# Linear attention and a long convolution in one kernel: normalising on the query exponentials, and the signal's spectrum stored by column group

## The chip, the cores and the metric

The kernel runs on one core of a Trainium2 chip, alone. The metric is the device time of one execution in microseconds. Engines are named as in the profile: PE (TensorE matmul) and PEld (its weight load), DVE (VectorE), ACT (ScalarE), POOL (GpSimd) and SP (SyncE, here only a queue that issues DMAs). One profiled execution gives the trace from which the single durations come.

## The reference

Two independent results are written side by side, 448 columns each, for 2048 rows.

```python
# A: linear attention, 16 heads of 28, softmax feature maps
qkv = (x @ wqkv) split into q, k, v per head
pq, pk = q @ w_phi, k @ w_phi                       # per head, 28 x 28
phi_q = concat(softmax(pq), softmax(-pq))           # over 28, bf16
phi_k = concat(softmax(pk), softmax(-pk))
kv = sum over rows of phi_k^T v ;  z = sum over rows of phi_k
o = (phi_q @ kv) / (phi_q . z + 1e-6)
a = o (heads concatenated) @ wo
# B: a diagonal state space model as a convolution
K[d, l] = Re sum_n C[d,n] * exp(dt[d]*A[d,n]*l) * dt[d]*B[d,n]      # 256 states, l < 2048
y = irfft(rfft(u padded to 4096) * rfft(K padded to 4096))[:2048] + u * Dskip
out = concat(a, y, axis=-1)
```

`exp(-pq)` and `exp(pq)` are each summed over the 28 features of a head, and the two halves of `phi_q` share one denominator; so a head's output of a row is two products of raw exponentials with `kv`, each times a scale of that row, head and half.

## The kernel before

**The planner.** The program is a list of units: each is a group of instructions with an engine (or two engines, of which the planner picks one), a cost, and what it reads and writes. `Plan.run` (line 214) goes through a simulated time with a list of units that are ready on each engine. It starts the unit that can start first; among those that can start within 0.02 us it takes the lowest rank from the table `RANKS` (line 105). `PHASES` (line 141) orders the stretches of ACT that need the same activation table. The result is a fixed order of instructions on each engine; on the chip every engine runs its own list in order and waits on semaphores. `copy` (line 439) evicts PSUM or copies SBUF on ACT or DVE, as the planner chooses; `tt` (line 416) is a product or sum of two tensors on DVE; `dma` (line 457) is given the queues from which the planner may choose. All SBUF tiles lie at fixed byte addresses in one large tile, so that tiles share memory by address, and the planner takes a later writer after all earlier readers.

**Stages.** B's kernel K is made from tables: eight chunks k of 56 channels, each with complex rotations (`rot`, sines on ACT), dampings (`exps`, exponentials on ACT, multiplied in by `damp` on DVE, two products and a negation `neg`), tables of high powers (`hi`, DVE) and `build`, a matmul of the two. Results of chunks 0 to 3, 4 to 5 and 6 to 7 are the column groups 0, 1 and 2 (224, 112 and 112 of the 448 columns); `scatter_k` (line 896, steps `sc0` to `sc2`) copies each group into `Kt` by some 44 small DMAs between SBUF places. `kernel_spectrum` (steps `ks`) transforms it with DFT tables `F`, streamed from DRAM through a ring of buffers.

`signal_spectrum` (line 672, steps `us`) transforms u early, in two blocks of 1024 rows; each of 16 steps evicts 128 x 896 numbers into one of two staging buffers `sg` and stores them to the DRAM tile `SUd` by one DMA. Late in the kernel `load_su` (line 973, steps `su0` to `su2`) loads them back by column group. For group 0 that reads pieces of 448 bytes of `SUd`, for groups 1 and 2 pieces of 224. Group 0's target `SUs[0]` is at `oU`, where the tables `U` of the even chunks were; it waits until chunk 6 is built. `conv_group` (line 1015) multiplies the two spectra on DVE (11 products and sums and 7 more per group), `skip` multiplies u (`UD`, loaded by four DMAs, here at `oEQ`) by Dskip, and `inverse` transforms back on PE with tables `GI`, adding u by an identity matmul.

**The attention.** Steps `key0` to `key15` accumulate `kv` and `z` on PE; `keyend` masks them into block-diagonal tiles `KVN` and `KVZ`. `query` (line 836) handles 512 rows at a time, sc = 0 to 3:

- `qe`: the projected queries are exponentiated on ACT, both signs, into `EQ` (112 x 2 halves x 4 groups of four heads x 512 rows). Channels are on partitions. Even and odd sc have a buffer each, at `oEQ` and `oG1`.
- `qz`: a matmul gives, with rows on partitions, the sum of exponentials and the product with z of each head and half. Five small DVE instructions turn these into the scales `SC` (128 rows x 4 x 2 x 16 heads, fp32).
- `q`, four times per sc, 128 rows each: eight matmuls give the unscaled products with rows on partitions, in two PSUM tiles (one per half). DVE multiplies each by the scales, spread over the 28 channels of a head, into bf16 tiles. Eight matmuls against the identity transpose the two and add them; the sum is evicted, four matmuls multiply by `wo`, and the result is evicted and stored.

Of the kernel before, what the change touches and what calls it, by code (L numbers as in the profile page):

```python
# [18 lines left out]
D_HEAD = 28  # L19
# [80 lines left out]
def pair_rows(x2, row, t, col):  # L100
# [4 lines left out]
RANKS = {"in": 76, "inAre": 129, "inAim": 160, "inCre": 137, "inBre": 274, "inCim": 272, "inBim": 280, "inx0": 84,  # L105
         "inx1": 209, "inx2": 217, "inx3": 227, "inqk": 141, "inG": 164, "inv_": 281, "one": 67, "pid": 139, "bd":
         124, "dt": 198, "stAre": 19, "stAim": 18, "amp": 265, "hl": 238, "cs128": 177, "cs32": 202, "cs64": 161,
         "stCre": 14, "stBre": 260, "stCim": 8, "stBim": 140, "cb": 230, "H32": 98, "H64": 35, "pw": 57, "xT0": 277,
         "xT1": 190, "xT2": 121, "xT3": 0, "fold1": 135, "fold0": 235, "vones": 49, "late0": 24, "late1": 259,
         "late2": 15, "zero": 206, "ua0.0": 147, "ab0.0": 136, "ua0.1": 143, "ab0.1": 59, "ua0.2": 123, "ab0.2": 148,  # L110
         "ua0.3": 252, "ab0.3": 88, "us0.0": 215, "us0.1": 3, "us0.2": 5, "us0.3": 30, "us0.4": 50, "us0.5": 219,
         "us0.6": 203, "us0.7": 48, "exps0": 271, "rot0": 70, "hi0.0": 42, "hi0.1": 192, "hi0.2": 46, "hi0.3": 105,
         "hi0.4": 263, "hi0.5": 196, "exps1": 257, "rot1": 183, "hi1.0": 34, "hi1.1": 81, "hi1.2": 37, "hi1.3": 110,
         "hi1.4": 158, "hi1.5": 261, "damp0": 233, "neg0": 207, "build0.0": 65, "build0.1": 255, "ua1.0": 131,
         "ab1.0": 269, "ua1.1": 16, "ab1.1": 226, "ua1.2": 248, "ab1.2": 106, "ua1.3": 78, "ab1.3": 182, "us1.0": 33,
         "us1.1": 166, "us1.2": 68, "us1.3": 262, "us1.4": 234, "us1.5": 97, "us1.6": 126, "us1.7": 1, "key0": 225,
         "key1": 80, "key2": 171, "key3": 239, "key4": 253, "key5": 167, "key6": 151, "key7": 91, "exps2": 276,
         "rot2": 77, "hi2.0": 178, "hi2.1": 61, "hi2.2": 29, "hi2.3": 279, "hi2.4": 231, "hi2.5": 111, "damp1": 211,
         "neg1": 107, "build1.0": 113, "build1.1": 28, "exps3": 201, "rot3": 208, "hi3.0": 267, "hi3.1": 174, "hi3.2":
         115, "hi3.3": 157, "hi3.4": 243, "hi3.5": 218, "damp2": 240, "neg2": 132, "build2.0": 138, "build2.1": 237,  # L120
         "key8": 216, "key9": 133, "key10": 118, "key11": 173, "key12": 89, "key13": 36, "key14": 116, "key15": 93,
         "keyend": 146, "exps4": 176, "rot4": 205, "hi4.0": 223, "hi4.1": 108, "hi4.2": 153, "hi4.3": 63, "hi4.4": 26,
         "hi4.5": 47, "damp3": 40, "neg3": 23, "build3.0": 128, "build3.1": 125, "kt5": 244, "sc0": 247, "exps5": 32,
         "rot5": 258, "hi5.0": 275, "hi5.1": 254, "hi5.2": 199, "hi5.3": 212, "hi5.4": 270, "hi5.5": 7, "damp4": 52,
         "neg4": 79, "build4.0": 200, "build4.1": 163, "qe0": 117, "qz0": 104, "q0.0": 112, "q0.1": 142, "q0.2": 222,
         "q0.3": 144, "qe1": 96, "qz1": 92, "q1.0": 11, "q1.1": 134, "q1.2": 31, "q1.3": 69, "exps6": 22, "rot6": 94,
         "hi6.0": 189, "hi6.1": 56, "hi6.2": 12, "hi6.3": 246, "hi6.4": 43, "hi6.5": 188, "damp5": 169, "neg5": 38,
         "build5.0": 159, "build5.1": 175, "sc1": 229, "exps7": 213, "rot7": 250, "hi7.0": 273, "hi7.1": 266, "hi7.2":
         85, "hi7.3": 102, "hi7.4": 120, "hi7.5": 165, "damp6": 75, "neg6": 64, "build6.0": 194, "build6.1": 181,
         "negid": 54, "gi": 101, "su0": 187, "qe2": 185, "qz2": 100, "q2.0": 152, "q2.1": 9, "q2.2": 21, "q2.3": 119,  # L130
         "qe3": 156, "qz3": 242, "q3.0": 25, "q3.1": 2, "q3.2": 122, "q3.3": 168, "f0.0": 45, "ks0.0.0": 27,
         "ks0.0.1": 55, "f0.1": 197, "ks0.1.0": 179, "ks0.1.1": 103, "f0.2": 145, "ks0.2.0": 149, "ks0.2.1": 245,
         "f0.3": 86, "ks0.3.0": 210, "ks0.3.1": 53, "f0.4": 264, "ks0.4.0": 214, "ks0.4.1": 71, "f0.5": 127,
         "ks0.5.0": 193, "ks0.5.1": 191, "f0.6": 249, "ks0.6.0": 17, "ks0.6.1": 114, "f0.7": 184, "ks0.7.0": 62,
         "ks0.7.1": 90, "damp7": 278, "neg7": 41, "build7.0": 51, "build7.1": 73, "ks1.3.0": 10, "ks1.3.1": 95,
# [12 lines left out]
class Plan:  # L148
# [64 lines left out]

    def run(self):
        units = self.units
        left, table, wire, lanes = {}, None, 0.0, {True: [0.0] * 8, False: [0.0] * 8}
        free = {e: 0.0 for e in self.LAT}
        ready = {e: [] for e in self.LAT}
        pe = {"warm": False, "win": 0.0, "busy": 0.0, "mode": 0}
# [147 lines left out]
def kernel(  # L367
# [84 lines left out]
    def mm(out_, lhsT, rhs, start, stop, **kw):  # L452
        nc.tensor.matmul(out_, lhsT=lhsT, rhs=rhs, start=start, stop=stop, **kw)  # L453
# [699 lines left out]
```

## Time and profile before

| | |
|---|---|
| three runs | 340.98, 341.71, 343.98 us; median 341.71 |
| the profiled execution | 343.51 us |
| its span, first to last instruction | 341.7 us |
| mean granted TensorE clock | 0.918 of full speed |
| DMA | 32.88 MB, 31062 packets |

The profile lists busy time by engine; windows give the same for stretches of the span. Groups collect instructions of one line, engine and shape: "out<-in partitions x elements, type, xcount | busy, mean ns of one | idle time of the engine just before them, and what ended it". Most operations are recorded by helpers, so that their line is that of `tt` (419), `act` (433), `copy` (443), `mms`' matmul (453) or `dma` (468), and shape and operands tell them apart; `mm`, `kb` and `arg` are PSUM tiles. The chain of waits follows the execution back from its last instruction, at each step to what released it. SPq is the queue of SP that issues DMAs; an issue that waits for data holds up all that stand behind it on its queue.

### The profile page before, as it was taken

Reading aid. Unit: us, or ns where it says so; the run is one execution under the profiler, and the core shown is the slowest. Engines: PE = TensorE matmul, PEld = TensorE weight load, DVE = VectorE, ACT = ScalarE, POOL = GpSimd, SP = SyncE. Lnnn points to the kernel's source line nnn. Section 1 sums busy time; section 2 is a strip of 40 time slices with the busy share of each in tenths; the row PEclk is TensorE's granted clock in tenths of the full one; section 3 lists DMA queues with packets and bytes.
Section 4 is the critical chain, followed back from the end, with each engine's and each line's share of the span. In section 5 each row is a group of like instructions: output and inputs, shape, how many; then the busy total and the mean of one; then the engine's idle time right before and its main releaser. Section 6 shows DMA issues by size and latency. Waiting matters only on the chain. (4 is left out here: it accounts for less than half of the span.)

```text
span 341.7 us, 9894 instructions
## 1 busy us (share of the span) xinstructions
PE 266.8 (78%) x4193; PEld 210.5 (62%) x4193; DVE 309.2 (90%) x438; ACT 254.2 (74%) x466; POOL 54.3 (16%) x99
## 2 busy tenths in 40 slices
PE   2536767888585989879997869998987686959984
PEld 1435743554563854755686647787775366949984
DVE  0578999999999999998999899999997979999992
ACT  4789999995999996986899999999976112214330
POOL 2100000000000000000019500007920035910000
PEclk9965579999899999998989998999998769999999
DMA  6994111221001002100203210322539968533333
GB/s 165 236 325 102 25 54 59 82 81 54 19 30 39 31 2 82 56 2 2 84 2 28 51 57 19 109 81 12 146 95 351 352 173 166 157 112 89 102 108 111
DMA packets 31062, 32.88 MB, mean 96 GB/s; under 512 B 8603, under 2 KB 29596, under 8 KB 30634
## 3 DMA queue, kind: packets, MB, share of 16 engines
q1 hardware_dynamic: 24338, 26.79, 25.9%
q0 software_dynamic: 3568, 4.26, 5.8%
q10 hardware_dynamic: 3112, 1.19, 1.6%
q8 instruction: 33, 0.54, 0.7%
q14 instruction: 11, 0.09, 0.1%
HBM read 24.28 MB, written 7.34 MB: 93 GB/s over the span
## 5 line engine op out<-in xcount | busy, mean ns | idle before, releaser
L453 PEld LDWEIGHTS <-sbuf 128*32 128x32 bf16 (+5 forms) x4049 | 196.2, 122 | 105.3 <-issue 52.5
L419 DVE TENSOR_TENSOR sbuf<-sbuf 128x448 bf16<-128x448 bf16 (+8 forms) x291 | 239.2, 872 | 7.0 <-ACT sbuf L433 3.1
L453 PE MATMUL mm<-sbuf 128*32 128x50 bf16 (+8 forms) x2151 | 144.7, 280 | 24.7 <-DVE sbuf L419 5.7
L433 ACT ACTIVATE sbuf<-arg 128x448 bf16<-128x448 f32 (+3 forms) x152 | 89.5, 710 | 0.0
L453 PE MATMUL kb<-sbuf 128*32 128x50 bf16 (+8 forms) x1152 | 74.7, 255 | 15.3 <-DVE sbuf L419 9.6
L443 ACT CAST sbuf<-mm 128x448 bf16<-128x448 f32 (+3 forms) x71 | 41.5, 599 | 25.2 <-PE mm L453 15.6
L453 PE MATMUL arg<-sbuf 128*128 128x112 bf16 (+1 forms) x746 | 49.0, 224 | 12.2 <-ACT sbuf L433 6.8
L468 POOL DMA_DIRECT2D sbuf<-sbuf x75 | 42.4, 594 | 92.0 <-ACT sbuf L443 90.4
L433 ACT ACTIVATE sbuf<-arg,sbuf 128x448 bf16<-128x448 f32 (+2 forms) x64 | 47.2, 738 | 0.8 <-PE arg L453 0.7
L443 ACT CAST sbuf<-kb 128x448 bf16<-128x448 f32 (+4 forms) x38 | 21.4, 572 | 20.7 <-PE kb L453 17.8
L433 ACT ACTIVATE sbuf<-mm 128x448 bf16<-128x448 f32 (+1 forms) x58 | 30.4, 604 | 8.0 <-PE mm L453 7.7
L809 DVE TENSOR_REDUCE sbuf<-sbuf 128x32 f32<-128x896 bf16 x16 | 17.2, 1072 | 1.2 <-ACT sbuf L433 1.2
L433 ACT ACT_TABLE_LOAD x12 | 15.4, 1283 | 3.5 <-issue 3.3
L633 PE MATMUL kb<-sbuf 128*112 128x128 bf16 x64 | 8.7, 310 | 10.2 <-DMA sbuf<-in_A_x_dram 7.8
L443 DVE CAST sbuf<-mm 128x448 bf16<-128x448 f32 (+3 forms) x22 | 13.2, 609 | 2.4 <-PE mm L453 2.4
L443 ACT CAST sbuf<-arg 128x224 bf16<-128x224 f32 (+1 forms) x13 | 4.6, 391 | 13.8 <-PE arg L453 13.8
L633 PEld LDWEIGHTS <-sbuf 128*112 128x112 bf16 x64 | 7.8, 208 | 11.3 <-DMA sbuf<-in_A_x_dram 8.4
L758 ACT ACTIVATE sbuf<-sbuf 128x1680 bf16<-128x1680 bf16 x8 | 13.9, 1732 | 0.7 <-DVE sbuf L419 0.7
L443 DVE CAST sbuf<-kb 128x448 bf16<-128x448 f32 (+2 forms) x15 | 9.2, 618 | 3.6 <-PE kb L453 1.9
L433 ACT ACTIVATE sbuf<-sbuf 128x896 f32<-128x896 f32 (+1 forms) x11 | 11.8, 1115 | 0.0
L419 DVE TENSOR_TENSOR sbuf<-kb,sbuf 128x448 bf16<-128x448 f32 (+3 forms) x19 | 9.9, 544 | 1.9 <-PE kb L453 1.8
L419 DVE TENSOR_TENSOR sbuf<-mm,sbuf 128x448 bf16<-128x448 f32 (+1 forms) x21 | 11.3, 566 | 0.4 <-PE mm L453 0.4
(35 smaller groups left out, 81.1 us busy)
## 6 DMA issues: line engine op xcount, KB each, us to landing
sbuf<-const SPq DMA_DIRECT2D x36, 224.0 KB
SUd<-sbuf SPq DMA_DIRECT2D x16, 224.0 KB
sbuf<-const SPq DMA_DIRECT2D x3, 1024.0 KB
sbuf<-in_A_x_dram SPq DMA_DIRECT2D x4, 448.0 KB
out_dram<-sbuf SPq DMA_DIRECT2D x16, 112.0 KB
sbuf<-in_B_u_dram SPq DMA_DIRECT2D x4, 448.0 KB
sbuf<-SUd POOLq DMA_DIRECT2D x1, 1792.0 KB, 17.9
sbuf<-SUd POOLq DMA_DIRECT2D x2, 896.0 KB, 10.0
```

Of the source, the lines that this page charges most:

```text
L419: lambda: nc.vector.tensor_tensor(out=at(out_), in0=at(a), in1=at(b), op=op), [whose(a), whose(b)], [out_])
L433: lambda: nc.scalar.activation(at(out_), at(a), func, scale=scale, **kw),
L443: lambda e: (nc.scalar.copy if e == "ACT" else nc.vector.tensor_copy)(at(out_), at(a)), [whose(a)], [out_])
L453: nc.tensor.matmul(out_, lhsT=lhsT, rhs=rhs, start=start, stop=stop, **kw)
L468: plan.add({e: own[e] for e in engs}, lambda e=engs[0]: QUEUES[e].dma_start(out=out_, in_=in_), r, w, lat=lat, load=pieces / 16000 * max(2 ...
L633: mms(p, [lambda t, j=j, x=x: nc.tensor.transpose(t[:, j, :], x[:, 112 * j:112 * j + 112], ident[:, :]) for j in range(4)], 0.4, [x, ident ...
L758: lambda en: nc.scalar.mul(m, m, -1.0) if en == "ACT" else nc.vector.tensor_scalar_mul(m, m, -1.0), [m], [m])
L809: plan.add({"DVE": 0.98}, lambda: nc.vector.tensor_reduce(zk[:, :, :], EK[:, :, :].rearrange("p s (h f) -> p s h f", f=D_HEAD), axis=AX.X, ...
```

## The change

**Attention.** The scales become bf16. Four transposes on PE put them with heads on partitions (32 x 512), a copy evicts them to `SCT`, one DMA stores them to a DRAM tile `SCd`, and four DMAs load them back, each row repeated over the 28 partitions of its head, and all twice the four groups, into `SCB` (112 x 2 x 4 x 512, one buffer for all sc). New steps `qo`: two DVE products per sc multiply `EQ` by `SCB` in place (112 x 2048 elements each, all bf16 in SBUF); eight matmuls of 512 columns then give the normalised output with channels on partitions, both halves added in PSUM; four copies evict it. Steps `q` keep only the product with `wo`, its eviction and the store.

**Spectrum of u.** `SUd` becomes two DRAM tiles, in which each column group is contiguous per partition; each of the 16 steps stores its numbers by three DMAs in place of one, and the loads read contiguous memory. `SUs[0]` and `UD` change places: `SUs[0]` lies where both `EQ` buffers are, `UD` at `oU`. The call of `load_su(0)` stands after the last two queries.

**Planner.** `RANKS` and `PHASES` are new throughout, so the order changes on all engines; three constants of the planner's DMA cost are some 5% larger, and its DMA time starts at 2.4 us. The load in `load_su` has another cost.

```diff
-RANKS = {"in": 76, "inAre": 129, "inAim": 160, "inCre": 137, "inBre": 274, "inCim": 272, "inBim": 280, "inx0": 84,
+RANKS = {"in": 44, "inAre": 15, "inAim": 123, "inCre": 130, "inBre": 168, "inCim": 134, "inBim": 273, "inx0": 61,
...
-        left, table, wire, lanes = {}, None, 0.0, {True: [0.0] * 8, False: [0.0] * 8}
+        left, table, wire, lanes = {}, None, 2.4, {True: [0.0] * 8, False: [0.0] * 8}
...
-    SUd = dram.tile([128, 2, 2, 2, 4, D_MODEL], BF16, name="SUd")
+    SUd = [dram.tile([128, 2, 2, 2, 4, 224], BF16, name="SUd0"), dram.tile([128, 2, 2, 2, 2, 4, 112], BF16, name="SUd1")]
+    SCd = dram.tile([4, 32, 512], BF16, name="SCd")
...
-                 load=pieces / 16000 * max(28 + 0.025 * piece, 0.0407 * piece))
+                 load=pieces / 16000 * max(29.4 + 0.0263 * piece, 0.0427 * piece))
...
-                    dma(["SP"], SUd[:, b, cp, st_, 2 * mp:2 * mp + 2, :], sg[:, :, :], r=[sg[:, :, :]],
-                        w=[("SUd", b, cp, st_, mp)])
+                    dma(["SP"], SUd[0][:, b, cp, st_, 2 * mp:2 * mp + 2, :], sg[:, :, 0:224], r=[sg[:, :, 0:224]],
+                        w=[("SUd", 0, b, cp, st_, mp)])
+                    for q in range(2):
+                        dma(["SP"], SUd[1][:, q, b, cp, st_, 2 * mp:2 * mp + 2, :], sg[:, :, 224 + 112 * q:336 + 112 * q],
+                            r=[sg[:, :, 224 + 112 * q:336 + 112 * q]], w=[("SUd", 1 + q, b, cp, st_, mp)])
...
-        SC = sb("SC", [128, 4, 2, 16], F32, oSC, bufs=2)
+        SC = sb("SC", [128, 4, 2, 16], BF16, oSC, bufs=2)
...
+        pt = ps(("mm", "kb"), [32, 4, 128], BF16)
+        mms(pt, [lambda t, t4=t4: nc.tensor.transpose(t[:, t4, :], SC[:, t4].rearrange("p s h -> p (s h)"), ident[:, :])
+                 for t4 in range(4)], 0.3, [SC[:, :, :, :], ident[:, :]])
+        SCT = sb("SCT", [32, 512], BF16, oSCT)
+        copy(SCT[:, :], (pt, lambda t: t[:, :, :].rearrange("p t x -> p (t x)")), 0.52e-3)
+        dma(["SP"], SCd[sc], SCT[:, :], r=[SCT[:, :]], w=[("SCd", sc)])
+        SCB = sb("SCB", [112, 2, 4, 512], BF16, oSCB)
+        for hh in range(4):
+            d = SCB[28 * hh:28 * hh + 28].rearrange("p s c x -> p (s c) x")
+            dma(["SP"], d, SCd[sc].rearrange("(k h) x -> h k x", h=4)[hh].unsqueeze(0).to_broadcast([28, 8, 512]),
+                r=[("SCd", sc)], w=[d])
+        oT = sb("oT", [112, 4, 512], BF16, oOT)
+        for cc in range(2):
+            step(f"qo{sc}.{cc}", rank)
+            e = EQ[:, :, 2 * cc:2 * cc + 2, :]
+            tt(e, e, SCB[:, :, 2 * cc:2 * cc + 2, :], ALU.mult)
+            for c in (2 * cc, 2 * cc + 1):
+                p = ps(("mm", "kb"), [112, 512])
+                mms(p, [lambda t, c=c, s=s: mm(t[:, :], KVN[:, s, c, :, :], EQ[:, s, c, :], s == 0, s == 1) for s in range(2)],
+                    0.45, [EQ[:, :, c, :], KVN[:, :, c]])
+                copy(oT[:, c, :], (p, lambda t: t[:, :]))
         for t4 in range(4):
-            ts = slice(128 * t4, 128 * t4 + 128)
-            on = []
             step(f"q{sc}.{t4}", rank)
-            for s in range(2):
-                pn = ps(("mm", "kb"), [128, D_MODEL])
-                mms(pn, [lambda t, c=c, s=s, ts=ts: mm(t[:, 112 * c:112 * c + 112], EQ[:, s, c, ts], KVN[:, s, c, :, :],
-                                                       True, True) for c in range(4)], 0.22,
-                    [EQ[:, s, :, ts], KVN[:, s]])
-                o = sb(f"on{s}", [128, D_MODEL], BF16, oON + 1792 * s, bufs=2)
-                tt(o.rearrange("p (h d) -> p h d", d=D_HEAD), (pn, lambda t: t[:, :].rearrange("p (h d) -> p h d", d=D_HEAD)),
-                   SC[:, t4, s].unsqueeze(2).to_broadcast([128, 16, D_HEAD]), ALU.mult)
-                on.append(o)
-            po = ps(("mm", "kb"), [112, 4, 128])
-            mms(po, [lambda t, c=c, s=s, o=on[s]: mm(t[:, c, :], o[:, 112 * c:112 * c + 112], ident[:, :], s == 0, s == 1)
-                     for c in range(4) for s in range(2)], 0.46, [on[0][:, :], on[1][:, :], ident[:, :]])
-            oT_ = sb("oT_", [112, 4, 128], BF16, oOT, bufs=2)
-            copy(oT_[:, :, :], (po, lambda t: t[:, :, :]))
             pf = ps(("mm", "kb"), [128, D_MODEL])
-            mms(pf, [lambda t, c=c, oT_=oT_: mm(t[:, :], oT_[:, c, :], wo[:, c, :], c == 0, c == 3) for c in range(4)],
-                0.77, [oT_[:, :, :], wo[:, :, :]])
+            mms(pf, [lambda t, c=c, t4=t4: mm(t[:, :], oT[:, c, 128 * t4:128 * t4 + 128], wo[:, c, :], c == 0, c == 3)
+                     for c in range(4)], 0.77, [oT[:, :, 128 * t4:128 * t4 + 128], wo[:, :, :]])
...
-    SUs = [group_tile("SU", i, o) for i, o in enumerate((oU, oE + 14336, oPID + 29184))]
+    SUs = [group_tile("SU", i, o) for i, o in enumerate((oEQ, oE + 14336, oPID + 29184))]
...
-    UD = sb("UD", [128, 2, 2, 4, D_MODEL], BF16, oEQ)
+    UD = sb("UD", [128, 2, 2, 4, D_MODEL], BF16, oU)
...
-        dma(["SP", "POOL"], SUs[gi].rearrange("p b c s m x -> p (b c s m) x"),
-            SUd.rearrange("p b c s m x -> p (b c s m) x")[:, :, 112 * q0:112 * (q0 + nq)],
-            r=[("SUd", b, cp, s, mp) for b in range(2) for cp in range(2) for s in range(2) for mp in range(2)],
-            w=[SUs[gi]], cost=1.7)
+        dma(["SP", "POOL"], SUs[gi].rearrange("p b c s m x -> p (b c s m x)"),
+            (SUd[1][:, gi - 1] if gi else SUd[0]).rearrange("p b c s m x -> p (b c s m x)"),
+            r=[("SUd", gi, b, cp, s, mp) for b in range(2) for cp in range(2) for s in range(2) for mp in range(2)],
+            w=[SUs[gi]])
...
-    load_su(0, 1700)
     query(2, 1790, 10, 1750)
     query(3, 1790, 10, 1750)
+    load_su(0, 1700)
```

## The prediction

> **What bounds the kernel now.** I read the busy times first, then windows by stage, then the groups with shapes kept apart, VectorE's instructions in order of time, the chain of waits and the queue that issues DMAs.
>
> ```profile
> span 341.7 us, 9894 instructions
> PE 266.8 (78%) x4193; PEld 210.5 (62%) x4193; DVE 309.2 (90%) x438; ACT 254.2 (74%) x466; POOL 54.3 (16%) x99
> ```
>
> The windows have start:end, length, then busy us (instructions) of each engine, the granted clock, DMA share and GB/s.
>
> ```profile
> 0.00:40.00 40.00, 18.93 (x165) 16.82 (x166) 24.52 (x36) 30.86 (x41) 3.78 (x14) 0.74 0.66 177
> 40.00:180.00 140.00, 116.20 (x1723) 80.50 (x1722) 137.39 (x207) 125.33 (x237) 4.53 (x11) 0.94 0.13 43
> 180.00:240.00 60.00, 52.09 (x945) 42.77 (x945) 57.09 (x89) 59.04 (x112) 19.52 (x35) 0.97 0.24 51
> 257.00:283.00 26.00, 19.82 (x268) 14.55 (x271) 21.74 (x30) 7.82 (x14) 3.39 (x2) 0.74 0.90 293
> 283.00:341.70 58.70, 45.22 (x772) 43.45 (x764) 51.50 (x59) 16.36 (x38) 13.76 (x24) 0.99 0.43 118
> ```
>
> VectorE (DVE, third) is the bound: 98% busy from 40 to 180 us, 95% to 240, and the fullest engine in the last stretch. It idles 15.5 us before 40 (data still coming in) and about 8 after the last convolution (output). What it stops doing in between comes off the span unless a wait takes its place. ScalarE (ACT, fourth) is a near second up to 257 us, so I check it too. In 257 to 283, DVE idles 4.3 us while the last queries are normalised piece by piece; a further 2.5 us of such gaps lie at 184 to 195 us and at 236.
>
> **What the arithmetic costs.** The groups (busy us, mean ns):
>
> ```profile
> L419 DVE TENSOR_TENSOR sbuf<-sbuf 128x1792 bf16<-128x1792 bf16 x58 | 60.5, 1082 | 0.6 <-ACT sbuf L443 0.2
> L419 DVE TENSOR_TENSOR sbuf<-sbuf 128x3584 bf16<-128x3584 bf16 x12 | 23.6, 2016 | 0.0
> L419 DVE TENSOR_TENSOR sbuf<-mm,sbuf 128x448 bf16<-128x448 f32 x18 | 10.6, 614 | 0.4 <-PE mm L453 0.4
> L419 DVE TENSOR_TENSOR sbuf<-kb,sbuf 128x448 bf16<-128x448 f32 x14 | 8.2, 607 | 1.9 <-PE kb L453 1.8
> L443 DVE COPY sbuf<-kb 112x512 bf16<-112x512 bf16 x9 | 3.6, 420 | 1.0 <-PE kb L633 0.9
> L443 DVE COPY sbuf<-sbuf 128x896 bf16<-128x896 bf16 x3 | 1.0, 345 | 0.0
> ```
>
> Successive instructions overlap a little, so I divide busy time by count. Removed: the 32 products that read PSUM, 10.6 + 8.2 = 18.8 us. Added: 8 products of 112x2048 elements, all bf16 in SBUF. From 60.5/58 = 1.04 us for 1792 elements and 23.6/12 = 1.97 for 3584 the slope is 0.52 ns per element, so 2048 take 1.18: 9.4 us. Added: four copies of the transposed scales (32x512), at the 112x512 row's 3.6/9 = 0.40: 1.6 us.
>
> Copies and negations go to whichever of ACT and DVE the planner finds free, and the built order of the changed kernel shows where. DVE takes four of the eight negations that ACT did. No such DVE instruction is in the trace: scaling the copy of 896 elements (0.33) from the 128-element scalar multiply (0.195) gives 0.47 for 1680, the two-tensor rate 0.98, so four cost 1.9 to 3.9; the copy is the nearer row (one source), so 1.9. It loses 4 evictions of 128x350 (0.53 each, -2.1) and 3 of folded weights (about 0.47, -1.4), and gains 2 of x's transposes (+0.8) and 4 others (0.6 each, +2.4): -0.3. DVE in all: -18.8 + 9.4 + 1.6 + 1.9 - 0.3 = **-6.2 us**.
>
> ACT: four negations fewer (4 x 1.73 = -6.9), 4 evictions of 128x350 more (+2.8), one activation-table load more (+1.3), other copies -1.6: about -4.4, of which some 3.9 before its last exponentials. PE has 208 matmuls fewer, 52 per query. So neither becomes the bound.
>
> **What is moved on the queues.** u's spectrum is stored by 48 DMAs in place of 16, 0.32 us of SP's issue each: 10 us more between 55 and 141 us, where the DMA share is 0.13 and SP mostly waits; the staging buffer is freed some 0.6 us later, and there are two of them. Without that cover, an eviction waits 0.6 us sixteen times. Its first load goes to the memory of the query exponentials, so it can't start before the last query's products on PE; before, it waited only for table 6.
>
> ```profile
> sbuf<-SUd POOLq DMA_DIRECT2D x1, 1792.0 KB, 17.9
> sbuf<-SUd POOLq DMA_DIRECT2D x2, 896.0 KB, 10.0
> ```
>
> These loads (KB, us to landing) moved pieces of 448 and 224 bytes at 100 GB/s, where 5-us windows around them show up to 366. The new ones are contiguous per partition; at 366 GB/s the first is 5.0 us plus a landing of some 2.5. In the built order DVE still has 18.6 us of work between the last query product and convolution 0 (copies 3.7, hi tables 2, damp 6 and 7 at 6.0 each, a negation). Off that go some 2 us for PE's products: 16.6 against 7.5, covered, with 9 us to spare. Table 6 now builds late, so u itself (UD) lands about 20.5 us after that product; it is wanted at 22.6 (after the first two products of convolution 0). That margin is 2 us.
>
> **The new wait** is the spread of the scales: store to DRAM, then four loads of 224 KB that wait for it on SP, then the product on DVE, with everything of DVE behind it. The nearest rows are a store of 112 KB and a load of 224 KB, both in the chain (start, us):
>
> ```profile
> 247.54 2.54 DMA out_dram<-sbuf
> ...
> 315.78 4.11 DMA sbuf<-const
> ```
>
> One trip: 0.4 issue + 2.5 + 4 x 0.43 + 4.1 = 8.8 us. Between the scales' copy and the product, DVE has in the built order over 12 us of other work for query 0, 9 for query 2, 7.9 for query 3. Query 1's loads wait instead for query 0's products, since the spread scales have one buffer: 5.8 us of loads under 5.8 us of work. So I charge 0.9 us; the bounds are 0 and the four trips bare, 35.
>
> The Trainium skill (DMA: Bandwidth & Descriptors, "Anatomy of one DMA") puts each DMA at about 2.0 us fixed plus bytes at 436 GB/s, and says the receipt of the write is most of the fixed part, worst towards HBM. As an estimate by that page a trip is 2 x 2.0 + 0.95 MB/436 GB/s = 6.2 us, and the charge would be 0. The trace's 2.54 and 4.11 us, for less data, lie above it, so the rows decide.
>
> Other new waits: ACT copies query 3's products and only then does the last exponentials, ending near 13.4 us after that product where DVE wants them at 11.6 (1.8); UD 0 to 4 (2.0); the qk weights stand 1.2 MB further back in the load queue, about 4 us, which delays VectorE's first power product from 21.6 to some 22.3 us (0.7); the last table is built some 3 us later against convolution 0, and the last kernel spectra came with 0.24 us to spare (0 to 2.4: 1.2). Sum with the 0.9: 6.6, against 4.3 + 2.5 = 6.8 of old gaps that go with the old instructions. I count them as equal.
>
> **The sum.** The profiled execution took 343.5 us, its span 341.7 and 1.8 around it: 343.5 - 6.2 = 337.3. It lies 1.8 above the median of the three times (341.71, from 340.98 to 343.98); for a median run I say 341.7 - 6.2 = **335.5**.
>
> **Rivals.**
> - *More gain* (15%). The old gaps go and the new waits find cover: 335.5 - 6.6 = 329. For it: ACT and PE have less to do. Against: the built order leaves DVE nothing else while it waits for the last exponentials.
> - *Slower: the trip through DRAM in front of the products* (18%). The queue bears it out:
>
> ```profile
> 178.09 9.49 SPq L468 DMA_DIRECT2D sbuf<-sbuf  x11
> 198.46 13.10 SPq L468 DMA_DIRECT2D out_dram<-sbuf  x4
> ```
>
> Eleven scatters of the kernel's tables hold SP 0.86 us each, and four output stores hold it 13 us, as each waits for its tile. In the built order such scatters and outputs stand around the store and loads of queries 2 and 3. With four in the way a trip is 8.8 + 3.4 = 12.2: stalls of 3.2 (query 2) and 4.3 (query 3), 3.4 for query 1, less the 0.9 charged: 10, and ACT's copies and the load behind query 3 pass on 1 to 2 more: 347. It decides once the stalls exceed 6.2 us. Against: the scatters start when their tables are ready, which is well before.
> - *The load of u's spectrum or UD late* (10%): 5.5 MB of loads in that stage take 15 us at 366 GB/s; a wait of 5 us gives 340.5.
> - *The products don't run at the bf16 rate* (7%), the change not doing what it says: the fp32 rows (2.02 us for 1792) make 2.3 each, 9 us more: 344.5.
> - The forecast, 50%, itself 332 to 340: negations +2.0, new waits 3 less or 3 more.
>
> Range 330 to 346: it leaves out some 5% below and 15% above. About 1% is what a measurement here can tell from no change, so faster is under 338.3 and slower over 345.1. Faster: 0.45 of the forecast, 0.15, and 0.02 of a smaller delay: 0.62. Slower: 0.16 of the queue rival and 0.02 of the products: 0.18. Same: 0.20.
>
> **What would show it.** Right: DVE busy near 303; the products at 1.18 us; the old gaps gone; under 4 us of DVE idle in front of the products and on the first spectrum load together. Wrong: DVE waiting on the DMA of the scales for several us per query, or on the last exponentials for much over 1.8, or a start whose 15.5 us of idle has grown.

## The result and the profile after

| | before | after |
|---|---|---|
| median of the runs on one chip | 342.3 us (340.98 to 343.98) | 362.25 us (361.77 to 363.32) |
| ratio, 95% interval | | 1.058 (1.053 to 1.064) |
| the profiled execution, its span | 343.51, 341.7 us | 361.77, 360.0 us |
| DMA packets, under 512 bytes | 31062, 8603 | 45434, 21899 |

The forecast was 335.5 us, its range 330 to 346. The kernel became 20 us slower. (Comparisons below are of undisturbed runs alone, so a ratio need not be that of the medians beside it.)

The busy times of the page of after:

```profile
span 360.0 us, 9525 instructions
PE 268.1 (74%) x3985; PEld 206.3 (57%) x3985; DVE 305.1 (85%) x421; ACT 250.9 (70%) x464; POOL 51.6 (14%) x100
```

DVE works 4.1 us less than before and the span is 18.3 longer, so DVE idles 22.4 us more. Windows say where. First after, then the two windows of before that match its last two (start:end, length, then busy us of PE, PEld, DVE, ACT and POOL, the granted clock, DMA share, GB/s): the third of after ends where the first product of convolution 0 begins on DVE, as the first of before does.

```profile
0.00:40.00 40.00, 19.76 (x189) 17.41 (x190) 22.66 (x32) 28.07 (x39) 3.66 (x12) 1.00 0.73 177
40.00:180.00 140.00, 109.75 (x1613) 74.96 (x1612) 137.81 (x203) 120.54 (x229) 13.09 (x26) 0.95 0.17 40
180.00:293.49 113.49, 84.73 (x1275) 62.81 (x1273) 90.30 (x131) 84.27 (x157) 21.62 (x40) 0.84 0.44 116
293.49:360.00 66.51, 53.89 (x916) 51.15 (x915) 54.35 (x58) 17.99 (x41) 13.27 (x23) 0.88 0.52 163
```

```profile
180.00:282.53 102.53, 86.00 (x1528) 69.28 (x1531) 95.37 (x138) 81.62 (x152) 32.27 (x52) 0.92 0.45 124
282.53:341.70 59.17, 45.69 (x792) 43.92 (x781) 51.97 (x59) 16.36 (x38) 13.76 (x24) 0.99 0.44 120
```

The length of a window less its third busy time is what DVE idled. The start has 17.3 us against 15.5, 40 to 180 us has 2.2 against 2.6, the last stage 12.2 against 7.2. The stage between, with the four queries, has 113.49 - 90.30 = 23.2 against 7.2: 16 of the 22.4 us lie there. DVE's instructions in that stage in order of time (start, busy us of a run of like instructions; in brackets the idle time before it and what ended that):

```profile
188.98 0.41 DVE L445 COPY sbuf<-kb 32x512 bf16<-32x512 bf16 x1 [0.79 <-PE kb L870]
...
194.94 1.89 DVE L421 TENSOR_TENSOR sbuf<-sbuf 128x3360 bf16<-128x3360 bf16 x1
201.84 2.79 DVE L421 TENSOR_TENSOR sbuf<-sbuf 112x2048 bf16<-112x2048 bf16 x3 [5.01 <-DMA sbuf<-SCd]
211.57 4.12 DVE L421 TENSOR_TENSOR sbuf<-sbuf 112x2048 bf16<-112x2048 bf16 x4 [1.60 <-DMA sbuf<-SCd]
...
244.54 0.62 DVE L445 CAST sbuf<-kb 128x448 bf16<-128x448 f32 x1 [2.48 <-DMA out_dram<-sbuf]
251.71 2.69 DVE L421 TENSOR_TENSOR sbuf<-sbuf 112x2048 bf16<-112x2048 bf16 x3 [3.21 <-DMA sbuf<-sbuf]
268.59 0.63 DVE L445 CAST sbuf<-kb 128x448 bf16<-128x448 f32 x1 [3.34 <-DMA out_dram<-sbuf]
```

Three of the four queries' first products wait, 5.0, 1.6 and 3.2 us, 9.8 in all; query 3's doesn't. The third wait is put down to a small DMA between SBUF places, but it stands in front of the product of query 2. The first two lines are the copy of query 0's scales and DVE's last work before it waits for them. Two evictions wait for output stores to leave their buffers. Query 0's trip can be followed on SP, which issues it (start, us of issue):

```profile
188.93 1.80 SPq L470 DMA_DIRECT2D sbuf<-const  x3
190.83 0.38 SPq L470 DMA_DIRECT2D SCd<-sbuf  x1
194.15 1.70 SPq L470 DMA_DIRECT2D sbuf<-SCd  x4
```

The scales' copy begins at 188.98 us, but SP first issues three loads of constants; the store goes out at 190.83 and lands 3.3 us later; the loads are issued from 194.15 and have landed at some 201.75, when the product starts. The chain of waits has the landing of the store and of the last load (start, us):

```profile
190.83 3.31 DMA SCd<-sbuf
...
195.44 6.28 DMA sbuf<-SCd
```

From the start of the copy, which takes 0.4, that is 12.8 us, where the prediction had 8.8 behind the copy. While those loads run, the DMA share is full and yet the engines move half of what they moved in a stretch of before. Two windows, of after and of before (last two columns: DMA share, GB/s):

```profile
198.00:200.00 2.00, 0.00 (x0) 0.00 (x0) 0.00 (x0) 2.00 (x4) 0.00 (x0) 0.50 0.99 187
```

```profile
258.00:262.00 4.00, 3.18 (x25) 2.70 (x25) 3.08 (x4) 1.91 (x2) 0.00 (x0) 0.57 1.06 384
```

PE and DVE both stand still in the first of them. So the theory to test was T1: the spread of the scales costs the time. Its rivals: the stores and loads of u's spectrum do, or the new order does. What in the spread would cost it was open: the products' wait, the store, the queue, or the loads themselves.

### The profile page after: what moved, and what is told of

The parts are those of the page before. It is cut to its first block, busy times and chain, and to the rows that moved or that the text cites. A ratio compares the mean times of both kernels' runs of the same rounds, so it can differ in the third digit from the quotient of the medians.

```text
span 360.0 us, 9525 instructions
## 1 busy us (share of the span) xinstructions
PE 268.1 (74%) x3985; PEld 206.3 (57%) x3985; DVE 305.1 (85%) x421; ACT 250.9 (70%) x464; POOL 51.6 (14%) x100
## 2 busy tenths in 40 slices
DMA packets 45434, 36.65 MB, mean 102 GB/s; under 512 B 21899, under 2 KB 44392, under 8 KB 44880
## 4 chain that ended last, share of the span: by engine, by line
PE 33%; ACT 14%; DMA 10%; DVE 8%; issue 3%; SPq 2%; ACTq 1%; DVEq 0%
PE mm L455 18%; ACT sbuf L435 10%; PE kb L455 9%; DVE sbuf L421 7%; PE arg L455 5%; DMA sbuf<-SCd 3%; DMA sbuf<-sbuf 3%; ACT sbuf L445 3%; SPq L470 2%; DMA SUd<-sbuf 2%; DMA sbuf<-const 2%; ACTq L470 1%; ACT L435 1%; DMA SCd<-sbuf 1%; DVE sbuf L445 1%
## 5 line engine op out<-in xcount | busy, mean ns | idle before, releaser
L421 DVE TENSOR_TENSOR sbuf<-sbuf 128x896 bf16<-128x896 bf16 (+9 forms) x299 | 248.5, 883 | 25.2 <-DMA sbuf<-SCd 6.6
L455 PEld LDWEIGHTS <-sbuf 128*32 128x32 bf16 (+5 forms) x3825 | 191.4, 124 | 122.4 <-issue 74.7
L455 PE MATMUL mm<-sbuf 128*32 128x50 bf16 (+7 forms) x2345 | 150.3, 282 | 30.7 <-ACT sbuf L435 9.5
L455 PE MATMUL kb<-sbuf 128*128 128x112 bf16 (+7 forms) x770 | 65.9, 268 | 20.7 <-DVE sbuf L421 17.4
L445 ACT CAST sbuf<-mm 128x448 bf16<-128x448 f32 (+4 forms) x76 | 40.7, 558 | 35.3 <-PE mm L455 29.1
L445 ACT CAST sbuf<-kb 128x448 bf16<-128x448 f32 (+3 forms) x35 | 18.8, 554 | 35.1 <-PE kb L455 24.6
L445 DVE CAST sbuf<-mm 128x448 bf16<-128x448 f32 (+1 forms) x24 | 14.6, 620 | 2.5 <-PE mm L455 1.9
L564 PE MATMUL mm<-sbuf 112*128 112x112 bf16 x48 | 5.5, 296 | 11.0 <-DMA sbuf<-const 7.4
L445 DVE CAST sbuf<-kb 128x448 bf16<-128x448 f32 (+1 forms) x12 | 7.6, 642 | 6.4 <-DMA out_dram<-sbuf 5.8
L445 DVE COPY sbuf<-kb 112x512 bf16<-112x512 bf16 (+2 forms) x16 | 6.4, 414 | 3.3 <-PE kb L636 2.2
```

What stands on the lines that cost most here:

```text
L421: lambda: nc.vector.tensor_tensor(out=at(out_), in0=at(a), in1=at(b), op=op), [whose(a), whose(b)], [out_])
L445: lambda e: (nc.scalar.copy if e == "ACT" else nc.vector.tensor_copy)(at(out_), at(a)), [whose(a)], [out_])
L564: mms(p, [lambda t, nch=nch, j=j: nc.tensor.transpose(t[:, nch, 112 * j:112 * j + 112], raw[nm][:, j, 128 * nch:128 * nch + 128], id112) f ...
```

## The experiments

Most kernels below keep the order of instructions: `dma` there takes, as `does`, the instruction to issue in place of its own, so that the planner sees the same units. Medians are given; the kernel before ran beside them in each group (342.84, 342.58, 343.26, 343.54, 343.03 us). The kernel after ran in another group, with 342.3 for before, so a difference to its 362.25 us compares two groups, and before's medians span 1.2 us.

### With and without the loads

**Loads left out, or left unread.** The product reads the memory of `H` in both, so the attention output lacks the scales. The first kernel has both hunks, the second the second one alone.

```diff
-                r=[("SCd", sc)], w=[d])
+                r=[("SCd", sc)], w=[d], does=lambda: None)
...
-            tt(e, e, SCB[:, :, 2 * cc:2 * cc + 2, :], ALU.mult)
+            SCR = sb("SCR", [112, 2, 4, 512], BF16, oH)
+            plan.add({"DVE": 0.065 + 2048 * 0.522e-3}, lambda e=e, v=SCR[:, :, 2 * cc:2 * cc + 2, :]: nc.vector.tensor_tensor(
+                out=e, in0=e, in1=v, op=ALU.mult), [e, SCB[:, :, 2 * cc:2 * cc + 2, :]], [e])
```

> The order on every engine stays; the sixteen loads of the spread scales are left out, and the products of the exponentials multiply by old contents of SBUF instead, so no product waits for DRAM. The changed kernel took 362.2 us. Theory 1, the round trip of the scales (waits in front of the products 9.8 us, output tiles whose stores stand behind the loads 5.8 us of VectorE's idle): 345 to 349. Theory 2, the new order itself (late tables, PE left cold, late u and last spectra): the loads matter little, 357 to 362.

> As the run without loads, but the sixteen loads are issued as before and nobody reads what they bring. What is left of the loss is then the queue: stores of the output tiles behind 917 KB of loads. If the waits in front of the products are all of theory 1: equal to the run without loads. If the queue matters as its share of the idle time says (5.8 of 15.6 us): about 352, some 5 above the run without loads.

Without loads: 345.17 us (344.04 to 347.44), ratio to before 1.004 (1.000 to 1.009). T1 holds: the loads cost 17 us by the medians (18 by the ratios). With the loads issued but read by nobody: 357.61 (two runs). So the products' waits, though they add up to 9.8 us in the trace, are worth 4.6; the other 12.4 us are what the loads do to everything else. (Loads that nobody reads don't wait for the last query's products either, so the 4.6 us hold that wait too.) The stage of the queries up to convolution 0, without loads and with unread loads:

```profile
180.00:277.39 97.39, 81.16 (x1281) 61.07 (x1280) 89.98 (x131) 83.74 (x158) 22.14 (x41) 0.90 0.33 98
```

```profile
180.00:290.89 110.89, 86.34 (x1285) 64.67 (x1285) 92.14 (x137) 86.05 (x162) 24.01 (x44) 0.85 0.44 119
```

DVE idles 7.4 us in the first and 18.8 in the second, with nothing to wait for in `SCB`. In its place DVE waits 5.1 us for output stores (2.5 without loads) and 4.0 for PE in front of a query's reciprocals (none without); in the next stage it waits 3.8 us for u (2.0). PE waits 4.5 us for constants (2.2 without).

**The loads cut to 128 bytes a partition,** still on SP behind the store:

```diff
+            src = SCd[sc][8 * hh, 0:64].unsqueeze(0).to_broadcast([28, 64])
-                r=[("SCd", sc)], w=[d])
+                r=[("SCd", sc)], w=[d], does=lambda v=SCB[28 * hh:28 * hh + 28, 0, 0, 0:64], src=src:
+                nc.sync.dma_start(out=v, in_=src))
```

> The kernel after with the 16 loads of scales cut to 128 bytes a partition, still issued on SP at their place and still waiting for the store; the products read other memory (H) of the same shape, so the attention output lacks the scales. Theory B (the loads cost by their bytes on the DMA engines): 344 to 348 us, as without loads (345.2). Theory W (SP, waiting for the store, holds up what is queued behind it): 354 to 358 us, as with the full loads unread (357.6).

346.36 us (344.44 to 348.81), ratio 1.010 (1.005 to 1.014): theory B. That SP waits for the store and holds up what is queued behind it costs next to nothing (1.2 us more than no loads, within the spread); the bytes cost the time.

### What in the bytes

**No wait for the store; one 8 KB piece a partition.** The first loads the same pattern from a constant in DRAM, so other numbers scale the attention. The second only sorts the scales by head first, so that a head's eight rows lie together.

```diff
+            src = F_d[0, 0:32, 0:4, :].rearrange("(k h) a b -> h k (a b)", h=4)[hh].unsqueeze(0).to_broadcast([28, 8, 512])
...
+            src = SCd[sc].rearrange("(h k) x -> h (k x)", h=4)[hh].unsqueeze(0).to_broadcast([28, 4096])
```

> The loads bring the same bytes in the same pieces, but from a constant in DRAM, so that they don't wait for the store of the scales (3.3 us landing at query 0); the products read what they bring. If the store's landing is most of the trip: 350 to 354. If the loads themselves are (6 us for 917 KB at about 190 GB/s): 357 to 360.

> The scales lie in DRAM so that each partition reads one run of 8 KB in place of eight of 1 KB; all else as in the changed kernel. If the pieces of 1 KB hold the loads at 190 GB/s, they run at about 366 and land some 2.5 us earlier: 353 to 357. If reading the same 32 KB 28 times is what is slow: no change, 361 to 363.

357.96 us (354.23 and 361.69: two runs far apart, so little follows but that it isn't the 17 us) and 357.61 (356.37, 358.86). The 8 KB pieces gain 4.6 us; neither is the whole cause. The loads still run at some 180 to 203 GB/s where nothing else runs beside them.

**Output stores on POOL's queue; each row its own.** Two kernels again, the second with a constant's rows in place of the scales and no wait for the store.

```diff
-            dma(["SP"], out2[r0:r0 + 128, 0:D_MODEL], of[:, :], r=[of[:, :]], w=[("out", r0)])
+            dma(["SP"], out2[r0:r0 + 128, 0:D_MODEL], of[:, :], r=[of[:, :]], w=[("out", r0)],
+                does=lambda r0=r0, of=of: nc.gpsimd.dma_start(out=out2[r0:r0 + 128, 0:D_MODEL], in_=of[:, :]))
...
+            src = F_d[0:8, 28 * hh:28 * hh + 28, 0:4, :].rearrange("i p a b -> p i (a b)")
```

> As the changed kernel (362.2 us), but the sixteen stores of the attention's output tiles are issued on POOL's queue, so that they no longer stand behind the loads of the scales on SP's. Leaving the loads out gave 345.2, leaving them unread 357.6: so 12 of 17 us come from what the loads do to others. If that is the stores behind them on the queue, which hold the two output tiles and with them ACT and VectorE: 350 to 355. If it is the DMA engines being full, whatever the queue: 359 to 362.

> The loads of the scales bring other data: each partition and piece its own 1 KB of a constant in DRAM, with no wait for the store; nothing is read twice. With 32 repeated rows of a constant the loads ran at some 190 GB/s with the DMA engines busy throughout. If reading the same rows over and over is what is slow: above 300 GB/s during the loads, and 350 to 353 us. If it is writing to 28 partitions at a time, or the pieces: 180 to 200 GB/s again, 354 to 358.

359.06 us: DVE's waits for output stores fell (one of 1.6 and one of 1.1 us were left), the products' stayed (4.3, 1.9, 3.1). 359.33 us with constant rows, all different: reading one row 28 times over isn't what makes it slow. These loads don't wait for the store either; by this run that wait is worth 2.9 us.

**112 partitions at a time from the four rows; the loads on POOL's queue.**

```diff
+            s2, c2 = hh // 2, hh % 2 * 2
+            src = SCd[sc].rearrange("(s h c) x -> s h (c x)", s=2, h=4)[s2, :, 512 * c2:512 * c2 + 1024]
+            src = src.unsqueeze(1).to_broadcast([4, 28, 1024])
...
-                r=[("SCd", sc)], w=[d])
+                r=[("SCd", sc)], w=[d], does=lambda d=d, hh=hh, sc=sc: nc.gpsimd.dma_start(
+                    out=d, in_=SCd[sc].rearrange("(k h) x -> h k x", h=4)[hh].unsqueeze(0).to_broadcast([28, 8, 512])))
```

> The kernel after with the same bytes of scales in the same number of DMAs, but each DMA writes all 112 partitions with 2 KB (one feature map and two head groups) instead of 28 partitions with eight times 1 KB; its order is kept. Theory P (a DMA into 28 partitions keeps the DMA engines busy at half their rate): the loads land within 3.5 us of their issue, at 350 GB/s or more, and the time falls to 349 to 353 us. Theory E (the bytes and the number of transfers set it, however they are spread): 356 to 360 us, as with the 8 KB pieces (357.6).

> The kernel after with the 16 loads of scales issued on POOL's queue instead of SP's, otherwise the same; its order is kept. Theory Q (SP's queue, in which stores, scatters and constants stand behind the loads): 348 to 353 us. If the DMA engines' time is what is short: 358 us or more, POOL's own scatters being late besides.

377.65 and 368.68 us: both were meant to help and both made it worse. The first didn't test its theory, and a window of it shows why:

```profile
202.00:204.00 2.00, 0.00 (x0) 0.00 (x0) 0.00 (x0) 0.21 (x1) 0.00 (x0) 0.50 0.26 101
```

A share of 0.26 is four of the sixteen DMA engines, at 25 GB/s each: a DMA whose source has four rows outermost ran on four engines. The trace's semaphore updates say the same: each of these loads lands in 4 parts, a load of after into 28 partitions in 14. The Trainium skill (DMA: Bandwidth & Descriptors, "Why a DMA increments its semaphore by 16 and not by 1") says this: the number of engines is the largest number up to 16 that divides the slowest dimension of both access patterns; the trace agrees, 4 for the 4 rows and 14 for the 28. In the second kernel POOL, which issues scatters of the tables too, waits for the stores in its turn (one such wait lasted 4.4 us).

**112 partitions at a time, a row for each.** A constant again, without a wait for the store, so that its counterpart is the run with distinct rows (359.33).

```diff
+            src = GI_d.rearrange("r p c m x -> (r p c m x)").rearrange("(p y) -> p y", p=256)
+            src = src[112 * (hh % 2):112 * (hh % 2) + 112, 1024 * (hh // 2):1024 * (hh // 2) + 1024]
+            s2, c2 = hh // 2, hh % 2 * 2
...
+                r=[("SCd", sc)], w=[d], does=lambda v=SCB[:, s2, c2:c2 + 2, :].rearrange("p c x -> p (c x)"), src=src:
+                nc.sync.dma_start(out=v, in_=src))
```

> The kernel after with the 16 loads of scales taken from a constant in DRAM, without a wait for the store, each into all 112 partitions, 2 KB from a row of its own (the attention is so scaled by other numbers); bytes, number of DMAs, place in the order and the products that read them are after's. Its counterpart is the run with distinct rows into 28 partitions at a time (359.3 us, some 190 GB/s with the DMA engines fully busy). Theory P (28 partitions at a time halve the rate of the DMA engines): 350 GB/s or more while the loads run, and 346 to 352 us. Theory E (these bytes cost the same however they are spread over partitions, if only all engines work): 356 to 360 us.

349.97 us (348.8 to 351.4), ratio 1.018 (1.012 to 1.024). The same bytes in as many DMAs at the same places cost 9.4 us less when each writes 112 partitions instead of 28. Not all of it need be the partitions: the pieces are 2 KB instead of 1 KB, where 8 KB pieces gained 4.6 us above, and each load lands in 16 parts instead of 14. The first products of the queries wait 1.7 us in all, instead of 7.2. A window of it, and the same one with 28 partitions:

```profile
196.00:198.00 2.00, 1.88 (x19) 1.68 (x20) 1.97 (x5) 2.00 (x5) 0.00 (x0) 0.50 0.83 214
```

```profile
196.00:198.00 2.00, 0.58 (x7) 0.50 (x5) 1.41 (x1) 2.00 (x5) 0.00 (x0) 0.50 1.01 180
```

Per full share that is 214/0.83 = 258 GB/s against 180/1.01 = 178 (at 242 to 244 us 288 GB/s at a share of 1.00). The 350 expected was too much, and at 242 to 244 us other transfers run too. DVE's idle time in the stage is 103.58 - 92.33 = 11.3 us with 112 partitions (window 180.00 to 283.58), and 111.96 - 90.87 = 21.1 with 28 (180.00 to 291.96). In one line, from after to no loads: 2.9 us for the store's wait, 9.4 for spreading over 112 partitions in 2 KB pieces, and 4.8 left to the same bytes so spread.

A rule that fits the 28 partitions stands in the Trainium skill (SBUF — State Buffer, "Door 1: The DMA port swizzle"): a transfer's rate depends on how many of SBUF's 16 DMA ports its partitions reach. By its table 28 partitions, from 0, 28, 56 or 84 on, reach 7 ports each; at its 27.2 GB/s a port this gives, as an estimate by that page, 190 GB/s. The 187 GB/s above and the 180 to 203 of the other runs lie around it. The same table lets 112 partitions reach all 16 ports, which by this rule of the Trainium skill would make, as an estimate, 16/7 = 2.3 times the rate; 258 against 178 is 1.4 times, so the ports were not shown to be the whole of it. That the DMA share is full meanwhile (0.99 to 1.01) is what the trace adds. The share can pass 1 (1.06 in the window of before), so it isn't a count of engines: here it is full with 14 to a load.

### u's spectrum

Three kernels with the order of before: u's spectrum stored and loaded by group; the stores split, the loads as they were; the loads contiguous (from a constant), the stores as they were.

```diff
-                        w=[("SUd", b, cp, st_, mp)])
+                        w=[("SUd", b, cp, st_, mp)], does=store)
...
+                    def store(sg=sg, b=b, cp=cp, st_=st_, mp=mp):
+                        for x0, x1 in ((0, 224), (224, 336), (336, 448)):
+                            nc.sync.dma_start(out=SUd[:, b, cp, st_, 2 * mp:2 * mp + 2, x0:x1], in_=sg[:, :, x0:x1])
...
-            w=[SUs[gi]], cost=1.7)
+            w=[SUs[gi]], cost=1.7, does=lambda e: QUEUES[e].dma_start(
+                out=SUs[gi].rearrange("p b c s m x -> p (b c s m x)"),
+                in_=GI_d.rearrange("r p c m x -> (r p c m x)").rearrange("(p y) -> p y", p=128)[:, 0:3584 * nq]))
```

> The kernel before with one part of the change alone: u's spectrum stored by three DMAs per step by column group and loaded contiguously, all in the old memory and the old order. The prediction counted the stores as hidden and the faster loads as worth little: 340 to 343 with 342.8 for the kernel before in the same job. If 48 small stores hold the evictions, 345 or more.

> The kernel before, with each of the 16 stores of u's spectrum issued as three DMAs (224, 112 and 112 columns) into the old layout; everything else, the order and the loads too, is before's. Of the 10 us that u's spectrum by group cost in before's order, theory S gives most to these stores (448 and 224 byte pieces that keep the staging tiles occupied): 349 to 353 us. Theory L gives most to the load, whose long pieces take the DMA engines from the transfers that PE waits for at the same time: 342 to 345 us here. S and L in equal parts: 346 to 348.

> The kernel before, its stores too, but the three loads of u's spectrum read 14336 and 7168 contiguous bytes a partition from a constant in DRAM instead of the stored spectrum (the convolution so gets other numbers). Theory L: 348 to 353 us, with PE waiting some 5 us for the constants around 262 us, and the first of the three loads landing in 9 instead of 18 us. Theory S: 340 to 344 us.

In the order of before the new layout costs: 353.16 us (348.97 to 354.89), ratio 1.024 (1.015 to 1.033). Of this the split stores alone make 347.16 (345.9 to 349.08), ratio 1.013 (1.007 to 1.018): between 120 and 160 us DVE idles 2.8 us instead of 0.7. The contiguous loads alone are no loss in the comparison (1.003; 0.999 to 1.007), but the ten runs spread from 341.5 to 355.33, so that isn't settled. With both, PE waits for the DFT constants while the first of those loads lands in 9.4 instead of 17.9 us; PE's waits in 240 to 285 us:

```profile
PE kb L454 <- DMA sbuf<-const: 5.3, 1, 5.3
```

The longest such wait of before in that stretch is 0.7 us. That the faster, less urgent load takes the engines from an urgent one is one reading, and not shown: this profile is of the longest of the four executions (354.89 us), and with the contiguous load alone, which lands in 10.6 us, PE's longest such wait is 1.2 us. What the two parts do together is left open.

The kernel after with the old layout and its own order:

```diff
-                    dma(["SP"], SUd[0][:, b, cp, st_, 2 * mp:2 * mp + 2, :], sg[:, :, 0:224], r=[sg[:, :, 0:224]],
-                        w=[("SUd", 0, b, cp, st_, mp)])
+                    dma(["SP"], SUd[0][:, b, cp, st_, 2 * mp:2 * mp + 2, :], sg[:, :, 0:224], r=[sg[:, :, 0:224]],
+                        w=[("SUd", 0, b, cp, st_, mp)], does=lambda sg=sg, b=b, cp=cp, st_=st_, mp=mp:
+                        nc.sync.dma_start(out=SUo[:, b, cp, st_, 2 * mp:2 * mp + 2, :], in_=sg[:, :, :]))
```

> The kernel after in its own order, with u's spectrum as in the kernel before: one store a step, the loads picked out of one tensor in 448 and 224 byte pieces. If u's spectrum by group costs after as much as it costs before (10 us): 351 to 354 us. If the later place of the first load and the fuller stage take that away: 359 to 363 us. The load of the first group then lands some 18 us after 276, at about 294, where the first product with it begins (293.5), so up to 3 us may be lost there in either case.

That changes nothing: 363.12 us (362.48 to 365.19) against 362.25. The 48 stores, which the chain of after runs through at 110, 116 and 122 us, drop out of the chain, 40 to 180 us gains 0.6 us, and the next waits take it back. So theories S (the stores) and L (the load) are about before's order only; of the 20 us, u's spectrum explains none.

### The order, and the rest

> The changed kernel with two of the planner's numbers set to what the trace shows: the store of the scales lands 3.3 us after its issue, and their loads take 1.9 times as long on the wire. The ranks stay, so only the order adapts. If the loss is an order that was made with too short a trip: 350 to 356. If the loads' occupation of the queue costs it whatever the order: 358 to 363.

> A version meant to be faster: the kernel after with the planner told what the trip of the scales takes (store 3.3 us, loads 1.9 times the wire), the scales loaded in one 8 KB piece a partition, and u's spectrum as in the kernel before; the planner orders it anew with the ranks of after. If the three add up (354.2 with the first, 4.6 us less by the pieces, up to 8 less by the spectrum): 342 to 346 us, and faster than before only if the reordering hides the trip altogether: below 341. If the costs overlap: 349 to 354.

```diff
-        dma(["SP"], SCd[sc], SCT[:, :], r=[SCT[:, :]], w=[("SCd", sc)])
+        dma(["SP"], SCd[sc], SCT[:, :], r=[SCT[:, :]], w=[("SCd", sc)], lat=3.3)
...
-                r=[("SCd", sc)], w=[d])
+                r=[("SCd", sc)], w=[d], slow=1.9)
```

With the planner told what store and loads take, and the same ranks, it orders the queries otherwise: 354.21 us, 8 less than after. The 8 KB pieces and the old layout of u's spectrum on top, ordered anew: 374.6 (372.0 to 377.4), 20 more. In a fixed order these two steps gained 4.6 us and cost nothing; what they share here is a new order from ranks that were not made for it. So the order is the likely cause, but the two steps were not taken apart, and no run holds the new order and leaves one of them out. No version was found that beats the kernel before.

**Without loads of scales and of u.** The convolution adds other numbers in place of u.

```diff
-            w=[UD[:, b, r, :, :]], cost=0.5, lat=3)
+            w=[UD[:, b, r, :, :]], cost=0.5, lat=3, does=lambda: None)
```

> The kernel after without the loads of scales (as in the run of 345.2 us; products on H's memory) and without the four loads of u into UD (the inverse transform adds other numbers). The wait for UD was 2.05 us there. If it costs what the timeline says: 342.5 to 344 us. If another wait is behind it (the spectra, the constants): 344.5 to 346.

345.38 us as the median of ten runs (340.46 to 348.22); the comparison gives 1.000 (0.994 to 1.005) against 1.004 without the loads of scales alone. The profiled spans are 340.6 and 343.2 us. That fits the 2 us of the wait for u, but the intervals overlap.

## Why the prediction was wrong

**The step that failed** is the one on the new wait: "One trip: 0.4 issue + 2.5 + 4 x 0.43 + 4.1 = 8.8 us ... So I charge 0.9 us". Its 4.11 us came from a load into 128 partitions, and was applied to four loads into 28 partitions each. Those run at 187 GB/s with the DMA share full: 0.92 MB take 4.9 us per query where 384 GB/s would take 2.4. The trip took 12.8 us for query 0: 1.9 for the copy and the loads of constants issued ahead of the store, 3.3 for the store instead of 2.9 with its issue, 7.6 for the loads instead of 5.8. The cover was too long as well: "over 12 us of other work for query 0" was 7.4 us on the chip, from the end of the copy at 189.39 to 196.83, so that even 8.8 us would have left a wait of 1.4. (For query 3, 7.9 were counted and 7.5 came; its product didn't wait, as 3.3 us of another wait lay in between.) But even with its true length the step would have missed most, because it charged the trip only to the product that waits for it. What the runs put in its place: 4.6 us for the waiting products and 12.4 for everything else that needs the DMA engines during the some 20 us (4 x 4.9) in which they are full. The 6.2 us that the prediction estimated by the Trainium skill (DMA: Bandwidth & Descriptors, "Anatomy of one DMA") and set aside for the rows was further off than the rows; that section is about DMAs that GpSimd issues, and these were issued by SP.

**The rival** of the trip in front of the products, with 18%, named the right place and the right side. That its 10 us of stalls came out as 9.8 is luck: it put 3.4, 3.2 and 4.3 us on queries 1, 2 and 3, and they were 5.0, 1.6 and 3.2 on queries 0, 1 and 2. It gave 347 because it priced stalls, not full engines. Scatters on SP's queue, its mechanism, were not the main part: small loads behind the same waits on SP took 346.4, and in front of the products the chain puts 1.3 us down to such a small DMA, at query 2.

**The arithmetic** held in the main. The added products, after:

```profile
L421 DVE TENSOR_TENSOR sbuf<-sbuf 112x2048 bf16<-112x2048 bf16 x8 | 9.8, 1222 | 9.9 <-DMA sbuf<-SCd 6.6 <-DMA sbuf<-sbuf 3.2
L764 DVE TENSOR_SCALAR sbuf<-sbuf 128x1680 bf16<-128x1680 bf16 x4 | 2.4, 592 | 0.0
```

1.22 us each against 1.18; the negations 0.59 against 0.47 (bounds 0.47 and 0.98). In all DVE's work fell by 4.1 us in the profiled run instead of 6.2; products and negations are 0.9 of the difference, and the rest was not itemised. The rival that the products miss the bf16 rate falls.

**Old gaps against new waits**, 6.8 for 6.6, "I count them as equal": not so, even with the trip taken away. Two windows without the loads of scales, the start and the last stage:

```profile
0.00:40.00 40.00, 19.44 (x183) 17.33 (x184) 22.42 (x32) 27.82 (x38) 3.64 (x12) 1.00 0.75 177
277.39:343.20 65.81, 52.20 (x916) 49.41 (x915) 54.34 (x58) 17.99 (x41) 13.28 (x23) 0.94 0.52 165
```

The span is 1.5 us longer than before's there: DVE's work falls by 309.2 - 304.4 = 4.8 us, and its idle time grows by 6.3, of which 2.1 at the start (17.6 against 15.5; 0.7 predicted) and 4.3 after convolution 0 begins (11.5 against 7.2; u and the last spectra, 2.0 + 1.2 predicted); the stage of the queries idles 7.4 against 7.2, so that the old gaps that were to go (4.3 + 2.5) were replaced in place. The wait for the last exponentials was 1.56 us, 1.8 predicted. With a trip that cost nothing, the change would have come out about even in this order. So of the 24.5 us between the forecast for the span (6.2 less) and what came (18.3 more), 16.8 are the loads (360.0 - 343.2), 6.3 are other waits and 1.4 are work that DVE didn't save.

**The queues.** The 48 stores as hidden: right for the time in after's order, by the run with the old layout, but not free: they stand in the chain, and in before's order they cost 4 us. The first load of u's spectrum landed in 7.8 us, at some 284, against 293.5 where it is wanted: the predicted 7.5 and 9 us to spare, as it came out. u was 2.6 us late (2.0 predicted).

```profile
sbuf<-SUd POOLq DMA_DIRECT2D x1, 1792.0 KB, 7.8
...
300.02 20.78 DVE L421 TENSOR_TENSOR sbuf<-sbuf 128x3584 bf16<-128x3584 bf16 x14 [2.57 <-DMA sbuf<-in_B_u_dram]
```

## What to carry to other kernels

Price a transfer into a slice of the partitions by a row with as few partitions: here 28 at a time ran at 178 GB/s per full share, 112 at 258. And a transfer costs twice: once where its reader waits, and once for every other transfer that meets it while the engines are full; the second was here nearly three times the first, and the run with the loads issued and unread tells them apart. Where a planner fixes the order, hold the order while one cost is tested, since a new order can move the time as much as the cost does.

## What was not expected of the hardware

- At a DMA share of 0.99 the loads into 28 partitions moved 187 GB/s, and at 1.06 a mix of loads into all of them 384 GB/s: the share doesn't show the rate.
- Neither 8 KB pieces (203 GB/s) nor distinct rows (180) raised the rate into 28 partitions much; a DMA with four rows outermost used 4 engines (101 GB/s). A load into 28 partitions landed in 14 parts, and one into 112 partitions, with a row for each, in 16.
- The granted clock was 0.62 in 180 to 200 us of after, where it was 1.00 before; without the loads it was 0.64, so they are not what lowered it.
